# Three up-weight loads on ScalarE's queue and a summed mean in an S5 scan with a GeGLU block

## The chip, the cores and the metric

One core of one Trainium2 chip. The metric is the device time of one execution in microseconds; the time before is the median of three runs.

The engines of the core work through queues of their own, each in order: TensorE (PE, matmuls and transposes into PSUM), VectorE (DVE), ScalarE (ACT), GpSimd (POOL) and SyncE (SP, which here only issues DMA transfers). They wait for each other by semaphores. A DMA transfer is issued by an instruction in some engine's queue and then runs on DMA engines beside it. ScalarE can issue transfers too: such an instruction stands in the same order as its arithmetic.

## What is computed

The input x has 2048 tokens of 512 features. Each token is layer-normalized; the result feeds a diagonal complex state-space scan (S5) and a GeGLU feed-forward block, whose SiLU gates the scan's output:

```
xn = _layernorm(x, axis=-1)
# S5: 512 complex states
Lam_bar = exp(dt * Lam);  dt = exp(log_dt)
Bu = einsum("bld,pd->blp", xn, ((Lam_bar - 1) / Lam)[:, None] * Bmat)
h  = Lam_bar * h + Bu[:, t, :]          # for t in 0..2047
s  = 2 * einsum("blp,dp->bld", h, Cmat).real + xn * Dskip
# GeGLU: 512 -> 1376 -> 512
g  = silu((gelu(xn @ w_gate) * (xn @ w_up)) @ w_down)
return x + s * g
```

All tensors are bfloat16.

## The kernel before

The tokens are cut into four slabs of 512, each slab into four tiles of 128 tokens. For a slab TensorE computes the up and gate products (`gate_tile`, L536), the down product (`down_pair`, L564), the input product of the scan (`half`, L615) and its output product (`y_part`, L579). The scan runs on VectorE, turned by a table of angles before and after (`half`, L627 to L659). ScalarE moves most products from PSUM to SBUF. The weights have four row tiles of 128 features (k = 0 to 3) and three column pieces of 512, 512 and 352 (c = 0 to 2).

The first slab is handled apart, since everything is still on its way. `center` takes the mean off each of its tiles: for tile 0 VectorE sums 320 of the 512 columns (L414, into `ma`) and ScalarE the other 192 (L411, into `mb`), and VectorE subtracts both in two pieces of 256 columns (L418). For tiles 1 to 3 ScalarE sums all columns (L423) and VectorE subtracts (L424). `head_t` transposes the centered tile on TensorE (L387 for tile 0 in two halves, L400 for the others) and copies it back into `xcT` (L391, L393, L402). `up_rows` then multiplies one tile, one row tile and one column piece at a time (L462), so that TensorE can start with the row tiles that have landed; the 352-column piece is done with all four row tiles at once (`first_w`, L499), and so are the gate products. The products are scaled with 1/sqrt(var) when they leave PSUM (L471, L505).

The weights come in pieces over SyncE's queue: three token tiles, then up row tile 0 (two halves of 512), the 352-column piece of all row tiles, row tile 1 and so on, the gate weights and the second slab (`load_x`, `load_w`, `load_slab`: L296, L287, L291). The three rows of parameters (log_dt, the imaginary and the real part of Lambda) are loaded over ScalarE's queue (L333), transposed (L672, L673), and make the angles (`angles`, L683 to L689) and the table (`tables`, L708).

No order is left to a compiler. Each call of `dve`, `acts`, `pe`, `pool` or `dma` adds a step with what it reads and writes to `Plan` (the costs given there have no effect on the program). `ORDER` is the order in which the steps are written out, and so each engine's own order; `SLOTS` says which buffer or PSUM bank each step's tile takes (six banks for whole products in `ps`, two in `pp`). The framework adds the semaphores. Each transfer signals its end on one of eight of them.

TensorE begins with seven products of constants (`dummies`, L375). The output of slab s is made tile by tile: `y_part` puts the skip term into the bank (L575), adds eight products (L579), multiplies by the gate (L585), adds x (L586) and stores (L589). The last tile of the last slab is done in two halves of 256 columns.

Of the kernel before, what the change touches and what calls it, by code (L numbers as in the profile page):

```python
# [45 lines left out]
)  # L46
SLOTS = {
# [4 lines left out]
    ),  # L52
    "pp": (
# [95 lines left out]
def kernel(  # L149
# [18 lines left out]
    P = 128  # L168
# [27 lines left out]
    def sb(name, shape, dt=BF16):  # L196
        return consts.tile(shape, dt, name=name)
# [722 lines left out]
```

## Time and profile before

| | |
|---|---|
| runs | 179.06, 178.76, 178.73 us |
| median | 178.76 us |
| span of the profiled execution | 176.9 us |
| median less span | 1.86 us |
| TensorE busy | 172.1 us (97%) |
| VectorE busy | 154.6 us (87%) |
| ScalarE busy | 132.6 us (75%) |
| moved by DMA | 18.66 MB |

The span runs from the first to the last instruction of one execution under the profiler; its own time outside the span isn't recorded, so the runs' median less the span stands for it. In the lines that follow, a timeline row gives start, duration in us, engine, source line, operation, tile written and read, shape and count; the bracket says how long the engine had been idle and what ended that. "SPq" and "ACTq" are issues of transfers. "PE" rows overlap: a matmul's duration is longer than the time until the next one starts. A row by stretches gives the stretch, its length, busy us and count of each engine (PE, PE's weight loads, DVE, ACT, POOL), TensorE's clock, the DMA engines' busy share and GB/s. The chain of waits follows the work that ended last back to the start: start, duration, who.

### The profile page before, as it was taken

What the parts mean: (1) busy time and instruction counts of PE and PEld (TensorE: products, weight loads), DVE (VectorE), ACT (ScalarE), POOL (GpSimd) and SP (SyncE); (2) the same over time, 40 slices, a digit from 0 to 9 for tenths busy, and PEclk for the clock granted to TensorE, in tenths of its full rate; (3) what the DMA queues carried; (4) which work ended last, traced back from release to release, by engine and by line L of the source; (5) the groups of instructions that cost most, each with busy time, mean ns of one, the idle gap of its engine ahead of it and who ended that gap; (6) DMA issues with size and microseconds to landing.
All of it is one profiled execution on the core that took longest, in us unless ns stands there. A gap on an engine that the chain in (4) does not pass through costs nothing.

```text
span 176.9 us, 2418 instructions
## 1 busy us (share of the span) xinstructions
PE 172.1 (97%) x834; PEld 82.3 (47%) x849; DVE 154.6 (87%) x253; ACT 132.6 (75%) x246; POOL 10.9 (6%) x25
## 2 busy tenths in 40 slices
PE   8999999999999999999999999999999999999992
PEld 2554544454454444444444444444444444444451
DVE  3743799999999988999999699999999999999343
ACT  6679999989999999956697665735898860793310
POOL 2640500000200000011000000000000000000000
PEclk9999999999999999999999999999999999999999
DMA  5999999997092730040057050063007300550531
GB/s 150 285 347 247 160 288 189 305 217 158 8 193 43 138 62 4 0 82 0 0 115 150 2 111 0 0 126 70 0 11 154 87 0 4 129 123 0 113 119 30
DMA packets 48467, 18.66 MB, mean 105 GB/s; under 512 B 40296, under 2 KB 48328, under 8 KB 48456
## 3 DMA queue, kind: packets, MB, share of 16 engines
q1 hardware_dynamic: 48432, 18.52, 46.7%
q8 instruction: 6, 0.10, 0.2%
q14 instruction: 5, 0.04, 0.1%
q10 hardware_dynamic: 24, 0.00, 0.0%
HBM read 6.46 MB, written 2.10 MB: 48 GB/s over the span
## 4 chain that ended last, share of the span: by engine, by line
PE 94%; DMA 2%; SPq 1%; issue 1%; DVE 0%
PE bank L536 31%; PE bank L564 21%; PE bank L615 16%; PE bank L579 16%; PE bank L499 7%; PE bank L462 3%; DMA wu<-in_B_w_up_dram 2%; SPq L296 1%; SPq L287 0%; DVE yg L585 0%; DVE ot L586 0%; PE bank L400 0%
## 5 line engine op out<-in xcount | busy, mean ns | idle before, releaser
L536 PEld LDWEIGHTS <-xnT 128*128 128x128 bf16 x288 | 28.1, 98 | 29.4
L564 PE MATMUL bank<-wd,atT 128*128 128x512 bf16 (+1 forms) x174 | 40.2, 379 | 0.1
L536 PE MATMUL bank<-wu,xnT 128*128 128x512 bf16 (+1 forms) x140 | 31.9, 356 | 0.1
L536 PE MATMUL bank<-wg,xnT 128*128 128x512 bf16 (+1 forms) x139 | 31.7, 356 | 0.3
L615 PE MATMUL bank<-xnT,BT 128*128 128x512 bf16 x128 | 30.9, 379 | 0.1
L646 DVE TENSOR_TENSOR_SCAN Fs<-rho,ini,W 128x512 bf16<-128x512 f32 x24 | 29.8, 1272 | 0.1
L579 PE MATMUL bank<-C,hst 128*128 128x512 bf16 (+1 forms) x134 | 29.7, 366 | 0.1
L564 PEld LDWEIGHTS <-atT 128*128 128x128 bf16 (+1 forms) x176 | 17.2, 98 | 20.3
L539 ACT ACTIVATE ubA<-bank 128x512 bf16<-128x512 f32 x24 | 14.6, 614 | 8.8 <-PE bank L536 8.3
L617 ACT ACTIVATE U<-bank 128x512 bf16<-128x512 f32 x32 | 19.1, 622 | 1.7 <-PE bank L615 1.7
L579 PEld LDWEIGHTS <-hst 128*128 128x128 bf16 x136 | 13.3, 98 | 14.0
L615 PEld LDWEIGHTS <-BT 128*128 128x128 bf16 x128 | 12.5, 98 | 14.3
L627 DVE TENSOR_TENSOR Q<-U,tab 128x4096 bf16<-128x4096 bf16 x8 | 18.3, 2287 | 0.7 <-ACT tab L715 0.6
L539 ACT ACTIVATE gtA<-bank 128x512 bf16<-128x512 f32 x24 | 14.8, 616 | 5.3 <-PE bank L536 4.6
L627 DVE TENSOR_TENSOR Q<-Fs,tab 128x4096 bf16<-128x4096 bf16 x8 | 18.3, 2285 | 0.1
L567 ACT ACTIVATE g<-bank 128x512 f32<-128x512 f32 x16 | 9.2, 594 | 12.1 <-PE bank L564 12.1
L585 DVE TENSOR_TENSOR yg<-bank,g 128x512 bf16<-128x512 f32 (+1 forms) x17 | 11.1, 655 | 5.0 <-PE bank L579 4.6
L539 ACT ACTIVATE ubB<-bank 128x352 bf16<-128x352 f32 x12 | 5.7, 475 | 6.6 <-PE bank L536 5.5
L838 ACT ACTIVATE junk<-x_tok 128x512 bf16<-128x512 bf16 x16 | 10.2, 649 | 0.0
L499 PE MATMUL bank<-wg,W 128*128 128x512 bf16 (+1 forms) x47 | 9.7, 356 | 0.1
L843 ACT ACTIVATE xna<-x_tok,nb,rs 128x512 bf16<-128x512 bf16 x12 | 9.6, 876 | 0.0
L575 ACT ACTIVATE bank<-sk 128x512 f32<-128x512 bf16 (+1 forms) x17 | 9.5, 577 | 0.1
(121 smaller groups left out, 190.0 us busy)
## 6 DMA issues: line engine op xcount, KB each, us to landing
out_dram<-ot SPq DMA_DIRECT2D x15, 128.0 KB, 1.8
x_tok<-in_A_x_dram SPq DMA_DIRECT2D x3, 512.0 KB, 5.6
wd<-in_B_w_down_dram SPq DMA_DIRECT2D x1, 1280.0 KB, 7.1
wg<-in_B_w_gate_dram SPq DMA_DIRECT2D x1, 864.0 KB
wu<-in_B_w_up_dram SPq DMA_DIRECT2D x6, 128.0 KB, 3.3
x_tok<-in_A_x_dram SPq DMA_DIRECT2D x4, 128.0 KB, 2.2
wg<-in_B_w_gate_dram SPq DMA_DIRECT2D x1, 512.0 KB, 7.8
wu<-in_B_w_up_dram SPq DMA_DIRECT2D x1, 352.0 KB, 3.9
```

The lines of the kernel that those rows point to most:

```text
L499: T.matmul(ps[:, 0 : b - a], lhsT=xcT[:, k, m * P : (m + 1) * P], rhs=wt[:, k, a:b], start=(k == 0), stop=(k == KT - 1))
L536: T.matmul(ps[:, 0 : b - a], lhsT=xnT[:, s % 2, m, k, :], rhs=wt[:, k, a:b], start=(k == 0), stop=(k == KT - 1))
L539: acts(b - a, lambda: act(out=dst, in_=ps[:, 0 : b - a], func=AF.Copy if up else AF.Gelu_apprx_tanh), [key], [ok], table=None if up else " ...
L564: T.matmul(ps[:], lhsT=atT[:fs, k, iT * P : (iT + 1) * P], rhs=wd[:fs, k, :], start=(k == 0), stop=(k == NFT - 1))
L579: T.matmul(ps, lhsT=hst[s % 2][:, j // NPT, j % NPT, m * P : (m + 1) * P], rhs=C2[:, j // NPT, j % NPT, c0:c1], start=False, stop=(j == 2 ...
L585: dve(w, lambda: V.tensor_tensor(out=yg[iy][:, 0:w], in0=ps, in1=g2[ig][:, c0:c1], op=ALU.mult), [key, ("g2", gg)], [("yg", gy)])
L615: T.matmul(ps[:], lhsT=BT[:, ri, k, pt * P : (pt + 1) * P], rhs=xnT[:, s % 2, :, k, :], start=(k == 0), stop=(k == KT - 1))
L617: acts(512, lambda q=q, ri=ri, ps=ps: act(out=U[ui][:, ri, q, :], in_=ps[:], func=AF.Copy), [key], [("U", ug, q, ri)])
L627: dve(4096, lambda: V.tensor_tensor(out=Qf, in0=src.unsqueeze(1).to_broadcast(WQ), in1=table, op=ALU.mult), reads, ["Q"], rate=2.0)
L646: pl.add(DVE, 1.12 if s == 0 else 1.185, lambda ri=ri, q=q, pt=pt, first=first: V.tensor_tensor_scan(out=Fs[:, ri, q, :], data0=rho[:, pt ...
L838: acts(512, lambda i=i, fn=fn, sc=sc, m=m: act(out=junk()[:], in_=x_tok[:, s * M + m, :], func=fn, scale=sc, accum_out=sx[:, s, i, m : m + ...
L843: acts(512, lambda m=m: act(out=xn[m], in_=x_tok[:, s * M + m, :], func=AF.Identity, scale=rs[:, s, m : m + 1], bias=nb[:, s, m : m + 1]), ...
```

## The change

Four things are changed:

- Up row tile 0 (both halves) and the second half of row tile 1 are loaded by ScalarE's queue instead of SyncE's.
- Of the parameter rows only log_dt stays on ScalarE's queue, ahead of these loads; the other two go to SyncE's.
- For tile 0, VectorE first adds the two partial means into a new `mc` (128x1), and then subtracts one scalar instead of two.
- `ORDER` and `SLOTS` are replaced as wholes: every engine's order and the choice of buffers differ over the whole kernel. There is one step more (693 for 692).

```
-    def load_w(nm, k0, k1, c0, c1, end, landed):
+    def load_w(nm, k0, k1, c0, c1, end, landed, act_queue=False):
         w, r = w_of[nm]
-        dma_sp(end, landed, lambda: nc.sync.dma_start(out=w[:, k0:k1, c0:c1], in_=r[:, k0:k1, c0:c1]),
-               [(nm, k, c) for k in range(k0, k1) for c in range(3) if c0 <= CH[c][0] < c1])
+        keys = [(nm, k, c) for k in range(k0, k1) for c in range(3) if c0 <= CH[c][0] < c1]
+        if act_queue:
+            dma(ACT, 0.43, landed - end, lambda: A.dma_start(out=w[:, k0:k1, c0:c1], in_=r[:, k0:k1, c0:c1]), writes=keys)
+            return
+        dma_sp(end, landed, lambda: nc.sync.dma_start(out=w[:, k0:k1, c0:c1], in_=r[:, k0:k1, c0:c1]), keys)
...
-    load_w("wu", 0, 1, 0, W1, 2.53, 4.4)
-    load_w("wu", 0, 1, W1, W2, 3.0, 4.95)
+    load_w("wu", 0, 1, 0, W1, 2.53, 4.4, act_queue=True)
+    load_w("wu", 0, 1, W1, W2, 3.0, 4.95, act_queue=True)
     load_w("wu", 1, 2, 0, W1, 3.47, 5.5)
-    load_w("wu", 1, 2, W1, W2, 3.94, 6.05)
+    load_w("wu", 1, 2, W1, W2, 3.94, 6.05, act_queue=True)
...
-        first = [dma(ACT, 0.48, 1.7, lambda t=t, v=v: A.dma_start(out=t, in_=v.rearrange("(k p) -> k p", p=P)),
-                     writes=[("pv", i)], rank=900.0, not_before=0.8, after=first)]
+        qe, qn = (A, ACT) if i == 0 else (nc.sync, SP)
+        dma(qn, 0.3, 2.4, lambda t=t, v=v, qe=qe: qe.dma_start(out=t, in_=v.rearrange("(k p) -> k p", p=P)), writes=[("pv", i)])
...
+    mc = sb("mc", [P, 1], FP32)
...
+            dve(1, lambda: V.tensor_tensor(out=mc[:, 0:1], in0=ma[:, 0:1], in1=mb[:, 0:1], op=ALU.add), [("ma", 0), "mb"], ["mc"])
             for i in range(2):
                 c0, c1 = i * HD, (i + 1) * HD
-                dve(HD, lambda c0=c0, c1=c1: V.tensor_scalar(out=xn[0][:, c0:c1], in0=x[:, c0:c1], scalar1=ma[:, 0:1], scalar2=mb[:, 0:1],
-                                                             op0=ALU.subtract, op1=ALU.subtract),
-                    [("x", 0, 0), ("ma", 0), "mb"], [("xc", 0, i)], rate=2.3)
+                dve(HD, lambda c0=c0, c1=c1: V.tensor_scalar(out=xn[0][:, c0:c1], in0=x[:, c0:c1], scalar1=mc[:, 0:1], scalar2=None, op0=ALU.subtract),
+                    [("x", 0, 0), "mc"], [("xc", 0, i)], rate=2.3)
```

The new heads of the queues that load, in order:

```
ACT: log_dt row; up k0 c0, up k0 c1; up k1 c1; partial mean of tile 0 (now L415)
SP:  x tiles 0, 1, 2; up k1 c0; up 352 columns, all k; x tile 3; up k2 c0; up k2 c1; Lambda rows;
     up k3 (1024 columns); gate 864 columns; gate 512 columns; second slab; Dskip;
     first xnT, then both transposed B; third and fourth slab; second xnT
```

In the new order TensorE has ten up products of row tiles 0 and 1 ahead of the 352-column products (six before), and the parameters' transposes come after those. VectorE's end of the order is: slab 2 tile 0 (multiply, add), then the last half tile of the last tile (multiply, add). The changed kernel's lines lie three or four further down: L415 is the partial mean on ScalarE, L420 the new sum, L423 the subtraction, L391 the transposes of tile 0, L503 the 352-column and first gate products, L583 the output products.

More of the change, by code (lines that the diff above doesn't have):

```diff
@@ L48 @@
     "ps": (
[3 rows of a table removed]
[3 rows of a table added]
     ),
     "pp": (
-        0, 1, 0, 1, 0, 1, 0, 1, 0, 0, 0, 1, 0, 1, 0, 1, 0, 1, 0, 1, 1, 0, 1, 0, 1, 1, 1, 0, 0, 0, 0, 1, 1, 0, 1, 0, 1, 0, 1,
+        0, 0, 1, 0, 0, 1, 1, 0, 1, 0, 0, 0, 1, 1, 0, 1, 0, 0, 1, 0, 0, 1, 1, 0, 1, 0, 1, 0, 0, 0, 1, 1, 0, 1, 0, 0, 0, 0, 0,
     ),
     "U": (
-        0, 1, 0, 2, 0, 1, 0, 2,
+        0, 1, 0, 2, 0, 1, 2, 0,
     ),
     "g2": (
-        5, 0, 1, 4, 3, 0, 4, 2, 2, 0, 1, 5, 3, 1, 4, 5,
+        4, 1, 0, 3, 0, 5, 3, 2, 5, 4, 5, 1, 2, 3, 1, 0,
     ),
     "at": (
-        2, 0, 1, 3, 2, 1, 0, 0, 0, 1, 2, 3, 2, 3, 0, 1,
+        0, 1, 3, 2, 0, 3, 2, 1, 3, 1, 1, 0, 2, 1, 2, 0,
     ),
     "gtA": (
-        0, 0, 1, 1, 0, 1, 0, 1, 1, 0, 0, 0, 1, 1, 0, 0,
+        1, 0, 0, 1, 0, 0, 0, 1, 0, 1, 1, 0, 0, 1, 1, 1,
     ),
     "gtB": (
-        1, 1, 0, 0, 0, 0, 1, 1, 1, 0, 0, 0, 0, 1, 0, 1,
+        0, 1, 0, 0, 1, 1, 1, 0, 1, 0, 0, 1, 0, 1, 0, 1,
     ),
     "ubA": (
-        0, 1, 0, 0, 1, 1, 1, 0, 0, 0, 1, 1,
+        0, 0, 1, 1, 0, 1, 1, 0, 1, 1, 0, 0,
     ),
     "ubB": (
-        0, 0, 1, 1, 1, 0, 0, 1, 0, 0, 1, 0,
+        0, 1, 0, 1, 1, 1, 0, 1, 0, 1, 0, 1,
     ),
     "yg": (
-        0, 0, 1, 1, 0, 1, 0, 1, 0, 1, 1, 0, 0, 0, 1, 0, 1, 0,
+        0, 1, 0, 1, 0, 0, 1, 1, 1, 0, 1, 0, 0, 1, 1, 0, 1, 0,
     ),
     "ot": (
-        1, 1, 1, 0, 1, 0, 0, 0, 0, 0, 0, 1, 1, 0, 1, 0, 1,
+        0, 1, 1, 0, 0, 0, 0, 1, 1, 0, 1, 0, 0, 0, 1, 0, 1,
     ),
     "sk": (
-        2, 3, 0, 1, 5, 7, 4, 6, 0, 1, 3, 2, 5, 4, 6, 7,
+        1, 2, 0, 3, 4, 7, 5, 6, 1, 2, 3, 0, 4, 6, 5, 7,
     ),
     "atT": (
-        0, 1, 3, 0, 1, 1, 3, 2, 0, 3, 2, 1, 1, 2, 3, 0,
+        0, 1, 3, 2, 3, 2, 2, 1, 3, 3, 1, 0, 2, 0, 2, 1,
     ),
```

54 rows, old and new, of tables (ORDER, SLOTS) are left out of this document.

## The prediction

> **What bounds the kernel now.** I read the page first (busy time, chain by engine), then the chain of waits in order of time, then the timeline by engine at both ends, then busy time by stretches.
>
> ```profile
> span 176.9 us, 2418 instructions
> ...
> PE 94%; DMA 2%; SPq 1%; issue 1%; DVE 0%
> ```
>
> TensorE carries 94% of the chain. The chain in order of time says from where:
>
> ```profile
> 3.06 3.89 DMA wu<-in_B_w_up_dram
> ...
> 6.99 1.35 PE bank L499 x8
> 8.35 0.43 PE bank L462 x2
> ...
> 172.01 1.76 PE bank L579 x16
> ```
>
> From 6.99 to 173.77 (172.01 + 1.76) no piece belongs to another engine. So three terms make the time: how much TensorE work is left at 6.99 (head), whether TensorE is starved later (body), and what follows its last matmul (tail). The span is 176.9, the median of the runs 178.76 us; the 1.86 us around the span stay as they are, and differences are added to 178.76.
>
> The head before, first the loads, then ScalarE, then VectorE, then TensorE's groups up to 7 us (count, busy us, mean ns):
>
> ```profile
> 0.79 0.55 ACTq L333 DMA_DIRECT2D pv<-in_A_log_dt_dram  x1
> ...
> 2.11 1.93 SPq L287 DMA_DIRECT2D wu<-in_B_w_up_dram  x4
> ...
> 3.90 0.66 PE L387 MATMUL bank<-ident,xna 128*128 128x128 bf16 x4
> ```
>
> ```profile
> 2.88 0.36 ACT L411 ACTIVATE junk<-x_tok 128x192 bf16<-128x192 bf16 x1 [0.67 <-DMA x_tok<-in_A_x_dram]
> 3.15 0.19 ACT L411 ACTIVATION_READ_ACCUMULATOR junk<-x_tok 128x1 f32 x1
> 3.44 0.63 ACT L423 ACTIVATE junk<-x_tok 128x512 bf16<-128x512 bf16 x1
> 3.97 0.19 ACT L423 ACTIVATION_READ_ACCUMULATOR junk<-x_tok 128x1 f32 x1
> 4.06 0.61 ACT L423 ACTIVATE junk<-x_tok 128x512 bf16<-128x512 bf16 x1
> ```
>
> ```profile
> 3.49 0.60 DVE L418 TENSOR_SCALAR xna<-x_tok,ma,mb 128x256 bf16<-128x256 bf16 x2
> 4.19 0.35 DVE L424 TENSOR_SCALAR xna<-x_tok,ma 128x512 bf16<-128x512 bf16 x1
> 4.46 0.28 DVE L391 COPY W<-bank 128x256 bf16<-128x256 bf16 x1
> ```
>
> ```profile
> L462 PE MATMUL bank<-wu,W 128*128 128x512 bf16 x6 | 1.6, 381 | 0.0
> L400 PE MATMUL bank<-ident,xna 128*128 128x128 bf16 x8 | 0.8, 222 | 0.1
> L387 PE MATMUL bank<-ident,xna 128*128 128x128 bf16 x4 | 0.7, 302 | 0.0
> ```
>
> ScalarE's part of the first mean starts when tile 0 arrives (2.88), the transposes at 3.90. By 6.99 TensorE has done twelve transposes and only six up products: it was short of tiles and weights.
>
> **The change part by part.** The listing of the changed program, with the semaphore that each instruction waits for, shows two waits that the diff doesn't:
>
> ```
> ACT 4 DMACopy wu_66<-in_B_w_up_dram 128x512 x2
> ACT 5 DMACopy wu_66<-in_B_w_up_dram 128x512 [waits DMAHW0_49]
> ACT 6 Activation junk1_116,mb_138<-x_tok_63 128x192
> DVE 2 TensorScalarPtr yg0_110,ma_137<-x_tok_63 128x320 [waits DMAHW0_49]
> PE 60 Matmult bank7_124<-wu_66,W_92 128x352 [waits DMAHW6_49]
> SP 9 DMACopy wu_66<-in_B_w_up_dram 128x1024 [waits DMAHW6_49]
> ```
>
> Loads share eight completion semaphores, and a load that reuses one waits for its last user. ScalarE's third load reuses that of token tile 0, so it goes out only when tile 0 has landed, and the partial mean stands behind it in ScalarE's order.
>
> *Head, ScalarE.* Such an issue on ScalarE isn't shown. Bounds: 0.43 (SyncE's four take 1.93, 0.04 between them) and 0.55 (ScalarE's first parameter row). I take 0.43 + 0.04, the same form of load. The parameter row and two loads end near 2.3; the third goes out from 2.88, the mean starts at 3.35 instead of 2.88, its accumulator is read by 3.81 (before 3.34), and VectorE follows 0.15 later, as it did at 3.49: 3.96.
>
> *Head, VectorE.* The new 128x1 sum isn't shown; the nearest row has 4 columns:
>
> ```profile
> 9.41 0.15 DVE L679 TENSOR_TENSOR a<-pf,dt__149 128x4 f32<-128x4 f32 x1
> ```
>
> With 0.04 to the next, dependent instruction: 4.15. The subtraction of one scalar from 256 columns lies between half of L424 (0.18: one scalar, 512 columns, 0.35) and L418 (0.34: two scalars, 256 columns, the second half entering 0.26 after the first); I take 0.21, near L424, which has the same form. First half 4.36, transposes 4.42 (they came 0.07 after L418's first half): 0.52 later than 3.90.
>
> *Head, TensorE.* The new order puts the copy of the first half ahead of tile 1's subtraction. Two transposes need 0.29 (0.22 and the next behind it), the copy 0.28: 4.75 to 5.03, first up product 5.13. Tile 1's mean is read at 4.63 (0.47 after the 4.16 of before), its subtraction runs 4.96 to 5.31, its transposes start at 5.37; tile 2's, 0.62 behind, at 6.02 once two products are through. Their copies (at most twice 0.28) end by 6.4 and 7.0, in time for products at 6.46 and 7.10. A product issues every 0.216 (8.35: two in 0.43), and so do four transposes (as many columns). So 5.13 one product, 5.37 transposes, two products, 6.02 transposes, seven products: the 352-column product begins at **7.75** with ten up products done. Before, it began at 6.99 with six and the parameters' two small transposes (0.1): 6.99 + 4 x 0.216 - 0.1 = 7.75. Head: **0.0**, from -0.47 (the mean isn't held) to +0.25 (issue 0.55, subtraction 0.34).
>
> So TensorE's early want of weights goes, and the wait takes the same amount back. The memory side has little to give (the last two columns are the DMA engines' busy share and GB/s):
>
> ```profile
> 3.00:4.00 1.00, 1.00 (x5) 0.11 (x2) 0.89 (x4) 0.91 (x4) 0.00 (x0) 1.00 0.90 264
> 4.00:5.00 1.00, 0.95 (x9) 0.45 (x8) 0.85 (x4) 1.00 (x5) 0.00 (x0) 1.00 0.78 194
> ```
>
> Only a fifth of one microsecond stands idle. The Trainium skill, DMA: Bandwidth & Descriptors, section "Issuing engines are not separate DMA queues", says that a second issuing engine saves issue time alone, since all transfers run on the same 16 engines. The shares agree, and by that rule alone the head would come out near 0 too.
>
> *Body.* TensorE's total is unchanged; after 7.75 it ends at 173.75 if it is fed. The times at which TensorE wants something, below, are sums of its rows along the new order from 7.75 on. I followed the hand-offs with these rows (ScalarE, then SyncE):
>
> ```profile
> 13.74 1.83 ACT L471 ACTIVATE at<-bank,rs 128x512 bf16<-128x512 f32 x3
> 15.59 1.28 ACT L505 ACT_TABLE_LOAD   x1
> ```
>
> ```profile
> 16.30 3.03 SPq L436 DMA_TRANSPOSE xnT<-xna  x1
> 19.38 2.42 SPq L314 DMA_TRANSPOSE BT<-in_A_B_im_dram  x1
> ...
> 25.91 2.98 SPq L436 DMA_TRANSPOSE xnT<-xna  x1
> ```
>
> ```profile
> DMA to landing us min/median/max: 4.9/5.3/5.8
> ```
>
> Tightest is ScalarE behind its table load. Its last piece of work before it ends near 16.1, the table is there at 17.4, eight evictions at most 0.57 apart (L471: three in 1.83) bring it to 21.97, and the one that frees the next bank ends at 22.4 to 22.5, where TensorE wants it (22.47). The second slab's transposed tokens leave at 25.9 as before and land 4.9 to 5.8 later (30.8 to 31.7); both orders want them at 31.45. The B transposes now follow the first xnT: the first takes xnT's place (16.30) and is wanted at 23.07, the second leaves as before (19.38) and is wanted at 25.66; by 5.8 both have room. Body: **+0.1**, from 0 to +0.4, since several margins are zero.
>
> *Tail.* In the new order VectorE has a whole other tile (slab 2, tile 0) right ahead of the last half tile:
>
> ```profile
> 169.74 0.69 DVE L585 TENSOR_TENSOR yg<-bank,g 128x512 bf16<-128x512 f32 x1
> 170.47 0.43 DVE L586 TENSOR_TENSOR ot<-yg,x_tok 128x512 bf16<-128x512 bf16 x1
> ...
> 173.79 0.42 DVE L585 TENSOR_TENSOR yg<-bank,g 128x256 bf16<-128x256 f32 x1
> ```
>
> TensorE ends that tile eight half products (0.88) before its last, at 172.9; yg starts at 172.97, ot 0.73 later at 173.70, and the last yg can enter 0.33 behind it (0.43 less the overlap): 174.03 instead of 173.79, and all behind it 0.24 later. Tail: **+0.24**, from 0 (the store hides it) to 0.4.
>
> The parameters' way over SyncE and the later memsets cost nothing, because VectorE waits for the second slab's tokens until 16.14 in any case; without that cover the chain of angles would cost some 0.3:
>
> ```profile
> 16.14 0.69 DVE L356 BATCH_NORM_STATS2 st<-x_tok 128x6 f32<-128x512 bf16 x1 [4.09 <-DMA x_tok<-in_A_x_dram]
> ```
>
> Sum: 178.76 + 0.0 + 0.1 + 0.24 = 179.10; with 0.05 for the loads behind the second wait (a tenth of rival 3's price), **179.15** (own range 178.85 to 179.45).
>
> **The rivals.**
> 1. *The mean isn't held.* ScalarE issues its third load without delaying the mean. For it: at 0.79 it issued while its table was still loading. Against: it would have to run past a semaphore. Head -0.47: 179.10 - 0.47 = 178.63.
> 2. *That, and a tail that hides.* The store of the other tile overlaps the last: 178.63 - 0.24 - 0.1 = 178.3.
> 3. *The last up rows come late: slower.* SyncE issues row tile 3 (SP 9) only once the 352-column load has landed, and the gate weights behind it. Such waits held nobody before; that load took 3.89 (3.06 to 6.95). Issued at 2.58 it lands at 6.5 to 7.0, and row tile 3 needs as long as any up load:
>
> ```profile
> DMA to landing us min/median/max: 2.2/3.5/3.9
> ```
>
> It lands between 8.7 and 10.9 and is wanted at 10.35; it decides from there on. Price up to 0.55: 179.7. Against: 3.5 is the time in a full queue, and at 7 us the queue has just run empty.
> 4. *TensorE's fast rate comes later: slower.*
>
> ```profile
> 0.76 3.15 PE L375 MATMUL bank<-const-bfloat16-1.0 128*128 128x512 bf16 x7 [0.76 <-PEq L904]
> ```
>
> Seven warm-up products take 3.15 (0.45 each, twice 0.216), the first transposes 0.30 and later ones 0.22: the fast rate comes after about 4.2. With TensorE idle from 3.91 to 4.42 it may come one such stretch (3.4) later, near 7.9; ten products at half rate until then cost 1.4: 180.5. The Trainium skill, TensorE: Matmul & The Clock Gate, Part 1, speaks of a free-running window of 3.4 us that has to be busy. The trace agrees with the length; whether the gap spoils the window no run shows.
>
> **How the numbers follow.** Forecast 0.45, rival 1 0.22, rival 2 0.10, rival 3 0.17, rival 4 0.06. About 0.2% (0.36 us) is what a measurement here can tell from no change. Faster (below 178.40): rival 2 and a third of rival 1, 0.17. Slower (above 179.12): 0.25 of the forecast, rivals 3 and 4, 0.48. The same: 0.35. The range 178.4 to 180.0 leaves out rival 4 and most of rival 2.
>
> **What would show it.** Right: the partial mean (now L415) starts near 3.35, the first transposes (L391) at 4.4, the first 352-column product (L503) at 7.7, TensorE's last matmul ends at 173.8 to 174.0, the last ot starts near 174.5. Wrong: the mean still starts at 2.9 (rival 1); TensorE idles ahead of the row tile 3 products near 10 us (rival 3); products after 5 us are 0.43 apart (rival 4); or TensorE has an idle stretch of over 0.3 us after 23 us.

## The result and the profile after

The changed kernel is slower: 181.09 us (median of 11 runs, 180.61 to 182.30) against 178.93 for the kernel before in the same runs, a ratio of 1.0112 (95%: 1.0079 to 1.0145). Two of the ten runs of one kernel below, parts_old_order (181.77 and 183.21 us), count as slow, being more than 1.5% over its fastest: its median of 180.42 holds them, and without them it is 180.15. The profiled execution of the changed kernel has a span of 179.1 us, 2.2 more than before. The page shows that TensorE no longer carries the chain alone:

```profile
span 179.1 us, 2413 instructions
...
PE 67%; ACT 14%; DVE 11%; DMA 4%; issue 3%; DVEq 0%; ACTq 0%
```

The chain of waits in order of time (start, duration, who) says where the others come in:

```profile
2.88 4.21 DMA wu<-in_B_w_up_dram
7.13 1.67 PE bank L466 x7
...
14.97 0.69 ACT at L475
...
38.69 0.50 ACT U L621
...
140.95 0.58 DVE yg L589
...
174.89 0.70 DVE yg L589
```

Three stretches of the new chain ahead of TensorE's last product are not TensorE's: a load at the start, ScalarE from 14.97 to 39.2, and VectorE ahead of 144.5. TensorE's timeline shows what each costs:

```profile
4.29 0.48 PE L391 MATMUL bank<-ident,xna 128*128 128x128 bf16 x4 [0.38 <-DVE xna L423]
4.96 0.39 PE L466 MATMUL bank<-wu,W 128*128 128x512 bf16 x1 [0.19 <-DVE W L395]
...
5.89 0.39 PE L404 MATMUL bank<-ident,xna 128*128 128x128 bf16 x4
7.13 1.67 PE L466 MATMUL bank<-wu,W 128*128 128x512 bf16 x7 [0.86 <-DMA wu<-in_B_w_up_dram]
8.64 1.36 PE L503 MATMUL bank<-wu,W 128*128 128x352 bf16 x8
9.83 0.59 PE L466 MATMUL bank<-wu,W 128*128 128x512 bf16 x2
10.36 0.17 PE L676 MATMUL bank<-ident,pv 4*128 4x4 bf16 x1
...
10.49 0.82 PE L466 MATMUL bank<-wu,W 128*128 128x512 bf16 x3
...
39.23 1.02 PE L540 MATMUL bank<-wu,xnT 128*128 128x512 bf16 x4 [0.20 <-ACT U L621]
...
144.49 1.02 PE L540 MATMUL bank<-wg,xnT 128*128 128x512 bf16 x4 [0.31 <-ACT gtA L543]
...
172.91 2.76 PE L583 MATMUL bank<-C,hst 128*128 128x512 bf16 x16
```

A row lasts until its last product has drained (0.38 for one of 512 columns), while the next could have been issued after 0.216. So an idle time in the brackets understates the loss by some 0.16. The three waits cost 0.86 + 0.16 = 1.02, 0.20 + 0.16 = 0.36 and 0.31 + 0.16 = 0.47 us. The first can be read from the starts too: four transposes from 5.89 take 0.22 and end at 6.11, and the next product starts at 7.13.

| term | predicted | measured | how |
|---|---|---|---|
| head | 0.0 | 1.02 | 352-column products at 8.64; before, with the same work done, 6.99 + 4 x 0.216 - 0.23 = 7.62 (the parameters' transposes, 10.26 to 10.49 here) |
| body | 0.1 | 0.88 | TensorE's last matmul ends at 175.67 (172.91 + 2.76), before at 173.77: 1.90, less 1.02 |
| tail | 0.24 | 0.27 | last yg at 175.96, before at 173.79: 2.17, less 1.90 |

Of the body's 0.88, the waits at 39.2 and 144.5 make 0.36 + 0.47 = 0.83. The head is that of one execution: of four further kernels below whose head is the same but for one product of constants more in one of them, three reach the 352-column products at 8.36 to 8.69, so it costs 0.7 to 1.1 in them too; the fourth, gate_sooner, is told below.

The tail's rows on VectorE, which is still busy with the other tile when TensorE is done at 175.67:

```profile
174.89 0.69 DVE L589 TENSOR_TENSOR yg<-bank,g 128x512 bf16<-128x512 f32 x1 [2.08 <-PE bank L583]
175.62 0.43 DVE L590 TENSOR_TENSOR ot<-yg,x_tok 128x512 bf16<-128x512 bf16 x1
175.96 0.42 DVE L589 TENSOR_TENSOR yg<-bank,g 128x256 bf16<-128x256 f32 x1
```

The wait at 39.2 comes from ScalarE's queue:

```profile
37.82 0.78 ACT L842 ACTIVATE junk<-x_tok 128x512 bf16<-128x512 bf16 x1
38.34 0.35 ACT L842 ACTIVATION_READ_ACCUMULATOR junk<-x_tok 128x1 f32 x1
38.43 0.75 ACT L621 ACTIVATE U<-bank 128x512 bf16<-128x512 f32 x1
```

Such a sum over 512 columns of the third slab takes 0.61 with its read-out (37.82 to 38.43). The new order has eight of them ahead of this eviction, the old one four in the same stretch, and the eviction frees the bank that TensorE wants next.

The wait at 144.5 is a loop over three engines, first VectorE's row, then ScalarE's:

```profile
141.78 0.68 DVE L522 TENSOR_TENSOR at<-gtA,ubA 128x1024 bf16<-128x1024 bf16 x1
```

```profile
142.54 1.28 ACT L543 ACT_TABLE_LOAD   x1 [3.16 <-DVE at L522]
143.84 1.08 ACT L543 ACTIVATE gtA<-bank 128x512 bf16<-128x512 f32 x2
```

VectorE's gate product reads a gate buffer (`gtA`) that ScalarE's next gate eviction overwrites. ScalarE has been idle for 3.16 us, yet it loads its table only after that wait, so the 1.28 us come on top.

### The profile page after: what moved, and what is told of

The parts are those of the page before. It is cut to its first block, busy times and chain, and to the rows that moved or that the text cites. A ratio compares the mean times of both kernels' runs of the same rounds, so it can differ in the third digit from the quotient of the medians.

```text
span 179.1 us, 2413 instructions
## 1 busy us (share of the span) xinstructions
PE 172.1 (96%) x833; PEld 82.3 (46%) x849; DVE 154.8 (86%) x254; ACT 130.2 (73%) x244; POOL 13.7 (8%) x25
## 4 chain that ended last, share of the span: by engine, by line
PE 67%; ACT 14%; DVE 11%; DMA 4%; issue 3%; DVEq 0%; ACTq 0%
PE bank L540 21%; PE bank L568 18%; PE bank L583 14%; PE bank L619 10%; DVE Fs L650 4%; PE bank L466 3%; ACT junk L842 3%; ACT gtA L509 3%; DVE Q L631 3%; DMA wu<-in_B_w_up_dram 2%; ACT U L621 2%; ACT at L475 2%; ACT xna L847 2%; DMA x_tok<-in_A_x_dram 1%; DVE yg L589 1%
## 5 line engine op out<-in xcount | busy, mean ns | idle before, releaser
L540 PE MATMUL bank<-wu,xnT 128*128 128x512 bf16 (+1 forms) x144 | 32.8, 357 | 0.3 <-ACT U L621 0.2
L619 PE MATMUL bank<-xnT,BT 128*128 128x512 bf16 x128 | 31.5, 379 | 0.0
L583 PE MATMUL bank<-C,hst 128*128 128x512 bf16 (+1 forms) x131 | 29.0, 366 | 0.3
L621 ACT ACTIVATE U<-bank 128x512 bf16<-128x512 f32 x32 | 19.6, 633 | 7.9 <-PE bank L619 7.9
L583 PEld LDWEIGHTS <-hst 128*128 128x128 bf16 x136 | 13.3, 98 | 14.0
L842 ACT ACTIVATE junk<-x_tok 128x512 bf16<-128x512 bf16 x16 | 11.1, 720 | 0.0
L503 PE MATMUL bank<-wg,W 128*128 128x512 bf16 (+1 forms) x47 | 10.1, 356 | 0.1
L466 PE MATMUL bank<-wu,W 128*128 128x512 bf16 x31 | 8.3, 379 | 1.1 <-DMA wu<-in_B_w_up_dram 0.9
```

What stands on the lines that cost most here:

```text
L466: T.matmul(ps[:], lhsT=xcT[:, k, m * P : (m + 1) * P], rhs=wu[:, k, a:b], start=(k == 0), stop=(k == KT - 1))
L540: T.matmul(ps[:, 0 : b - a], lhsT=xnT[:, s % 2, m, k, :], rhs=wt[:, k, a:b], start=(k == 0), stop=(k == KT - 1))
L583: T.matmul(ps, lhsT=hst[s % 2][:, j // NPT, j % NPT, m * P : (m + 1) * P], rhs=C2[:, j // NPT, j % NPT, c0:c1], start=False, stop=(j == 2 ...
L619: T.matmul(ps[:], lhsT=BT[:, ri, k, pt * P : (pt + 1) * P], rhs=xnT[:, s % 2, :, k, :], start=(k == 0), stop=(k == KT - 1))
L621: acts(512, lambda q=q, ri=ri, ps=ps: act(out=U[ui][:, ri, q, :], in_=ps[:], func=AF.Copy), [key], [("U", ug, q, ri)])
L842: acts(512, lambda i=i, fn=fn, sc=sc, m=m: act(out=junk()[:], in_=x_tok[:, s * M + m, :], func=fn, scale=sc, accum_out=sx[:, s, i, m : m + ...
```

## The experiments

My theory (T) after reading the trace was that the head waits for weights that land late, that the new order makes the two later waits by itself, and that the tail is as predicted. The rivals are named in the expectations, which were written before the runs. An edit of the order is shown by step numbers: in ORDER, steps 0 to 2 and 7 are the loads of the token tiles, 3 and 4 those of up row tile 0, 5 and 6 of row tile 1 (6 is ScalarE's third load), 8 and 9 of row tile 2, 10 of row tile 3, 11 the 352-column load, 25 to 27 the parameter rows, 30 the partial mean. Unless said otherwise the base is the changed kernel. "Ratio" is against the kernel before in the same runs; the changed kernel's is 1.0112.

| kernel | median us | ratio (95%) | span |
|---|---|---|---|
| load_after_mean | 182.35 | 1.0180 (1.0135 to 1.0225) | 180.1 |
| up11_on_sync | 180.42 | 1.0074 (1.0053 to 1.0095) | 178.6 |
| order_alone | 180.59 | 1.0084 (1.0063 to 1.0105) | 178.5 |
| parts_old_order | 180.42 | 1.0078 (1.0044 to 1.0112) | 177.2 |
| sum_later | 181.24 | 1.0132 (1.0096 to 1.0168) | 178.9 |
| gate_sooner | 181.33 | 1.0126 (1.0094 to 1.0157) | 179.4 |
| tail_halves | 182.02 | 1.0170 (1.0142 to 1.0198) | 179.2 |
| eight_warmups | 180.89 | 1.0106 (1.0085 to 1.0127) | 178.8 |
| parts_old_order_warm | 179.49 | 1.0028 (1.0015 to 1.0041) | 177.7 |
| mc_alone | 179.11 | 0.9999 (0.9984 to 1.0014) | 177.4 |
| old_order_two | 179.67 | 1.0047 (1.0021 to 1.0073) | 177.4 |
| three_mended | 179.45 | 1.0033 (1.0016 to 1.0050) | 177.4 |
| wide_load_later | 181.57 | 1.0110 (0.9915 to 1.0305) | 180.7 |

### Is it the held mean or the late load?

**load_after_mean**

```
-    ... 3, 2, 4, 5, 6, 30, 45, 11, 7 ...
+    ... 3, 2, 4, 5, 30, 6, 45, 11, 7 ...
```

> Kernel: the changed one, with ScalarE's third load (up row tile 1, second half) put behind the partial mean in ScalarE's order; nothing else. Theory T (late weights): of the changed kernel's 2.16 us, 1.03 are TensorE's wait for this load, which lands at 7.09 because the 352-column load (360 KB) was issued ahead of it; 0.36 (at 39.2) and 0.47 (at 144.5) are waits that the new order makes by itself; 0.26 is the tail. By T the mean starts at 2.9 and the first transposes at 3.9, but the load still lands at 7.1 or later (it now waits for token tile 1), TensorE still waits for it, and the time stays within 0.2 us of the changed kernel's 181.09 (up to 0.4 slower). Rival H (the hold): the 0.39 by which the mean is late is what costs; then this kernel is 0.4 us faster, 180.7.

The mean now starts at 2.92 and the transposes at 4.07, but the load (chain of waits) lands later still, and TensorE (timeline) waits for it:

```profile
3.48 4.60 DMA wu<-in_B_w_up_dram
```

```profile
5.67 1.16 PE L466 MATMUL bank<-wu,W 128*128 128x512 bf16 x2
...
8.11 1.67 PE L466 MATMUL bank<-wu,W 128*128 128x512 bf16 x7 [1.05 <-DMA wu<-in_B_w_up_dram]
```

Issued 0.60 later, it lands at 8.08 instead of 7.09. Undoing the hold gained nothing, and rival H is out; in the changed kernel, too, TensorE still waits 0.86 for the load after the held mean. The loss is larger than T allowed (span +1.0, up to 0.4 expected), and all of it is the load's: the row at 8.11 stands 0.98 later than that at 7.13.

**up11_on_sync**

```
-    load_w("wu", 1, 2, W1, W2, 3.94, 6.05, act_queue=True)
+    load_w("wu", 1, 2, W1, W2, 3.94, 6.05)
```

> Kernel: the changed one, with up row tile 1's second half issued by SyncE, behind its first half and ahead of the 352-column load. By T the load lands near 5.5 to 5.9 instead of 7.09, TensorE has no wait for it (its 352-column products begin at 7.2 to 7.7 instead of 8.64), and the time falls by 0.9 to 1.3 us to 179.8 to 180.2; the waits at 39 and 144 us stay, a us earlier. Rival H: only the hold goes, -0.4, 180.7. Rival O (the loss lies in the new order alone, and the head only moves waits about): less than 0.3 us comes off, since the later waits grow by what the head gains.

TensorE doesn't wait for this load any more; its 352-column products start at 7.94, 0.70 sooner. They were expected from 7.2 on, and what now sets the time is token tile 2, for whose sum ScalarE waits; before the change that sum started at 4.06 without a wait:

```profile
5.03 0.63 ACT L427 ACTIVATE junk<-x_tok 128x512 bf16<-128x512 bf16 x1 [0.78 <-DMA x_tok<-in_A_x_dram]
```

```profile
7.94 1.36 PE L503 MATMUL bank<-wu,W 128*128 128x352 bf16 x8
```

The later waits are there as T has them, at 38.70 and 143.95, 0.53 and 0.54 sooner than in the changed kernel. The other 0.16 goes between 10.45 and 12.12, where four transposes and six products take 1.67, in the changed kernel 1.52 (11.15 to 12.67). With 0.5 of the span T's size was missed by about half; its mechanism is what the rows show.

**wide_load_later**

```
-    ... 45, 11, 7, 8, 9 ...
+    ... 45, 7, 8, 11, 9 ...
```

> Kernel: the changed one, with the 352-column load (360 KB) put behind token tile 3 and the first half of row tile 2 in SyncE's order. ScalarE's third load now shares its semaphore with token tile 1, so it goes out, and the mean starts, some 0.5 later than in the changed kernel (near 3.4 and 3.8). Theory T (order on the 16 DMA engines): with 128 to 256 KB instead of 360 ahead of it the third load lands 2.8 to 3.4 us after its issue instead of 4.21. Rival Q (a load that ScalarE issues in the middle of the stream is slow in itself, whatever is ahead): 4.0 to 4.6 again. The time is no test here: the mean comes later and so do the 352 columns; 180.5 to 181.8.

The profile's summary of ScalarE's three loads (the changed kernel, then this one):

```profile
DMA to landing us min/median/max: 3.0/3.6/4.2
```

```profile
DMA to landing us min/median/max: 3.1/3.1/3.1
```

The summary holds the landings that the profile ties to an issue, two of the three in each kernel. Here both come 3.1 us after the issue, that of the third load, issued at 3.58, too; in the changed kernel the 4.2 is the third load's. So a load of ScalarE's isn't slow in itself, and rival Q is out.

What counts is all that is ahead of it, not the 352-column load alone (352 KB; 360 in the expectations, in thousands of bytes). Added up from the issues and landings, 768 KB of token tiles and weights issued earlier have not landed here when the third load goes out, 864 KB in parts_old_order and parts_old_order_warm (below), where the 352-column load is among them too, and 992 KB in the changed kernel and in load_after_mean. The load takes 3.1 us here, 3.4 and 3.7 with 864 KB, 4.2 and 4.6 with 992 KB, and 3.9 to 4.3 in four further kernels with 992 KB. Nor does it wait until the 352 columns are there: in the changed kernel it lands at 7.09, and they, issued at 2.58, took 5.0.

### Parts and order apart

**order_alone**

```
-    load_w("wu", 0, 1, 0, W1, 2.53, 4.4, act_queue=True)
+    load_w("wu", 0, 1, 0, W1, 2.53, 4.4)
 the other two loads likewise
...
-        qe, qn = (A, ACT) if i == 0 else (nc.sync, SP)
+        qe, qn = A, ACT
...
-    ... 25, 1, 3 ... 9, 26, 27, 10 ...
+    ... 25, 26, 27, 1, 3 ... 9, 10 ...
```

> Kernel: the changed kernel's order, buffers and summed mean, but all loads of weights issued by SyncE and all three parameter rows by ScalarE, as before the change. By T the mean isn't held and row tile 1 comes ahead of the 352 columns, so TensorE waits less in the head: only for the 352-column load, which now goes out behind everything at 4.4 and lands near 8; 180.1 to 180.8, with the two later waits in place. Rival H: 180.7. Rival I (issuing from ScalarE saves SyncE's time and is worth that much; without it the head gets worse): 181.4 or more. Rival O: 181.0 within 0.2.

180.59, within T's range; in the profile TensorE's last row stands 0.54 earlier than in the changed kernel. SyncE alone serves the new order no worse than both queues. TensorE's wait for weights is still there, smaller, and its 352-column products begin at 8.09. T named the wrong load for it: it isn't the 352-column load, for which TensorE doesn't wait here, but one of the 128 KB loads ahead of it:

```profile
6.14 0.38 PE L466 MATMUL bank<-wu,W 128*128 128x512 bf16 x1 [0.59 <-DMA wu<-in_B_w_up_dram]
```

Both later waits stand at 38.70 and 143.95, so they belong to the order. Rival I is out. H forecast the same time; it falls by load_after_mean.

**parts_old_order**

```
 ORDER, SLOTS: those of before, with the new sum (step 32, later steps one number up) and,
 with the parameters' transposes (38, now 39) moved too,
-    ... 25, 1, 26, 2, 27, 3, 4, 30, 31, 11, 44, 32, 6 ... 62, 38, 71, 70, 10, 39 ...
+    ... 25, 1, 2, 3, 4, 6, 30, 31, 11, 26, 27, 45, 32 ... 63, 72, 71, 10, 39, 40 ...
```

> Kernel: everything of the change but its order and buffers: the order of before, with the three loads on ScalarE's queue in the place that they have in the changed kernel, two parameter rows on SyncE's behind the 352-column load, the parameters' transposes put just ahead of their copy, and the summed mean. By T the old order needs six products ahead of the 352 columns, which are loaded early here, and row tile 1 only later, so nothing waits for the third load: 178.6 to 179.2, with no wait of TensorE near 39 or 144 us. Rival H: 179.3 (the mean is held all the same). Rival I' (loads from ScalarE's queue are slow in themselves): 179.9 or more.

The profiled execution agrees with T: 177.2, no wait of TensorE behind the head, 352-column products at 7.29 (before: 6.99, with the same work ahead). The median doesn't, and by the time alone this would be rival I'; but in the profile ScalarE's loads take 2.6 to 3.4 us, no longer than SyncE's before (2.2 to 3.9), so they are not slow in themselves. The ten runs lie between 179.02 (the profiled one) and 183.21. That is the widest spread so far, and two further kernels were made for it (below); what the later runs lost no profile shows.

**mc_alone**

```
 on the kernel before:
+            dve(1, lambda: V.tensor_tensor(out=mc[:, 0:1], in0=ma[:, 0:1], in1=mb[:, 0:1], op=ALU.add), [("ma", 0), "mb"], ["mc"])
-  ... scalar1=ma[:, 0:1], scalar2=mb[:, 0:1], op0=ALU.subtract, op1=ALU.subtract) ...
+  ... scalar1=mc[:, 0:1], scalar2=None, op0=ALU.subtract) ...
```

> Kernel: the one before with the summed mean alone. By the measured rows the new sum (0.16) costs more than the two-scalar subtraction saves (0.06): the transposes of tile 0 come 0.10 to 0.15 later than 3.90; behind them TensorE waited 0.24 for the 352-column load at 6.99 in any case, so the time stays within 0.15 us of before. Theory W adds that the idle stretch of 0.1 may delay the fast rate in some runs. Rival M (the sum costs its full 0.19 all the way, since the two-scalar subtraction isn't dearer): +0.2.

No change (0.9984 to 1.0014). The transposes start at 4.01, 0.11 later, and TensorE waits for the 352 columns behind them in any case:

```profile
7.50 1.35 PE L500 MATMUL bank<-wu,W 128*128 128x352 bf16 x8 [0.26 <-DMA wu<-in_B_w_up_dram]
```

```profile
4.36 0.63 ACT L424 ACTIVATE junk<-x_tok 128x512 bf16<-128x512 bf16 x1 [0.32 <-DMA x_tok<-in_A_x_dram]
```

These rows also show how far the same loads in the same queues move between executions: the 352 columns come 0.5 later than in the kernel before (6.99), and the sum of token tile 2, for which ScalarE now waits, 0.3 later (4.06).

### The two later waits and the tail

These edits are worth less than the runs' spread, so TensorE's positions in the profile decide, not the medians. By the medians all three kernels are slower than the changed one (181.24, 181.33 and 182.02 for 181.09), so none of the gains that T forecast came out in time.

**sum_later**

```
-    ... 441, 298, 141, 313, 303, 201, 314 ... 318, 364, 304 ...
+    ... 441, 298, 141, 313, 201, 314 ... 318, 364, 303, 304 ...
```

> Kernel: the changed one, with the last of ScalarE's eight sums over the third slab's tokens that stand ahead of the scan's eviction at 38.4 us moved some five us later in ScalarE's order. Theory T: TensorE's wait at 39.2 comes from ScalarE's queue, which is full from 15 us on and holds these sums (0.61 each) ahead of an eviction whose bank TensorE wants; without one of them the eviction comes 0.61 sooner and the 0.36 go: span 178.7 to 178.8 (179.1), time 0.3 to 0.4 lower, and TensorE's wait near 144 us stays. Rival O (a wait taken away here comes back at the next tight place): the wait at 144 grows by what goes here, time within 0.15 of 181.09. Rival D (ScalarE is late because of transfers): the wait at 39 stays.

TensorE's wait at 39 is gone, so ScalarE's queue was its cause. But only part of the 0.36 is kept. The row that stands at 144.49 in the changed kernel starts at 144.29, and 0.10 of these 0.20 come from the head (352-column products at 8.54 for 8.64). In between a hand-off takes over in which ScalarE waits for VectorE:

```profile
44.16 0.60 ACT L543 ACTIVATE gtA<-bank 128x512 bf16<-128x512 f32 x1 [0.26 <-DVE at L522]
```

It comes at 44.24 in the changed kernel, 0.08 later, so it hardly moves with what ScalarE gains. That is rival O, though at 44, not at 144.

**gate_sooner**

```
-    ... 553, 539, 550, 551, 536, 533, 607, 623, 552 ...
+    ... 553, 550, 551, 536, 607, 623, 539, 533, 552 ...
```

> Kernel: the changed one, with two skip terms on VectorE (slab 3, tiles 2 and 3; 0.33 each, at 138.3 and 141.5 us) put behind the two gate products at 141.9 and 142.5. Theory T: VectorE is full from 122 to 142 us; its gate product frees the buffer that ScalarE's next gate eviction writes, and ScalarE's table load of 1.28 stands behind that wait, then comes the eviction that frees TensorE's bank. With 0.66 less ahead of it the table load starts near 141.9 and TensorE's wait of 0.47 at 144.5 goes; span 178.6 to 178.7, time 0.4 to 0.5 lower. Rival P (the table load doesn't depend on the wait, something else holds it): the wait at 144.5 stays and the time with it.

The wait at 144.5 is gone; down products and gate products follow each other (11 x 0.216 = 2.38 from 142.45):

```profile
142.45 2.54 PE L568 MATMUL bank<-wd,atT 128*128 128x512 bf16 x11
144.82 1.03 PE L540 MATMUL bank<-wg,xnT 128*128 128x512 bf16 x4
```

The execution is longer all the same, for a reason in its head:

```profile
7.31 2.29 PE L466 MATMUL bank<-wu,W 128*128 128x512 bf16 x7
9.43 0.31 PE L503 MATMUL bank<-wu,W 128*128 128x352 bf16 x1
```

The seven products that took 1.67 at 7.13 take 2.29 here, and the 352 columns begin 0.79 later. TensorE's last row starts at 173.25, 0.34 after that of the changed kernel: 0.81 more at 40.04, 0.47 less at 144. That the wait isn't gone merely because TensorE comes late is shown by three_mended (below), which has the same edit and an early head; there the gate products follow without a wait too:

```profile
142.85 1.03 PE L540 MATMUL bank<-wg,xnT 128*128 128x512 bf16 x4
```

**tail_halves**

```
-    ... 679, 669, 689, 661 ... 670, 690, 671, 691, 675, 680, 692, 672 ... 641, 683, 573, 642, 643, 644, 684 ...
+    ... 679, 669, 661 ... 670, 671, 675, 680, 672 ... 641, 689, 683, 573, 642, 643, 644, 690, 691, 692, 684 ...
-    ot = [sb(f"ot{i}", [P, D]) for i in range(2)]
+    ot = [sb(f"ot{i}", [P, D]) for i in range(2)] + [at[0][:, 0:D]]
```

> Kernel: the changed one, with both halves of the last tile at the very end of TensorE's and VectorE's order, so that no whole tile stands right ahead of the last half; the store that this half would have waited for gets an output buffer of its own. Theory T: the last multiply enters as soon as TensorE is done instead of 0.23 to 0.26 later: span 178.8 to 178.9, time 0.2 to 0.3 lower. Rival S: the extra half on VectorE and its store take the same room: no change within 0.1.

No gain: by the profile, rival S. Its "no change" doesn't fit the time, though: four of the five runs lie at 181.93 to 182.10, only the profiled one (180.93) near the changed kernel's 181.09, and what the four lost stays open. Two halves after a whole tile leave the last one behind just as much:

```profile
175.34 0.42 DVE L589 TENSOR_TENSOR yg<-bank,g 128x256 bf16<-128x256 f32 x1
175.80 0.29 DVE L590 TENSOR_TENSOR at<-yg,x_tok 128x256 bf16<-128x256 bf16 x1
176.01 0.42 DVE L589 TENSOR_TENSOR yg<-bank,g 128x256 bf16<-128x256 f32 x1
```

TensorE ends at 172.10 + 3.64 = 175.74, the last yg enters at 176.01, 0.27 later, as in the changed kernel. In the old order a down product (2.38) stands between the last whole tile and the halves, and gives VectorE its time.

### When TensorE gets fast

**eight_warmups**

```
-    dummies(7)
+    dummies(8)
```

> Kernel: the changed one, with eight products of constants at the start instead of seven. The changed kernel's runs lie 1.7 us apart (180.61 to 182.30), those of before 0.47 but for one; in the profile of the kernel with the load behind the mean TensorE's up products took 0.63 instead of 0.38 up to 6.6 us. Theory W: TensorE's idle stretch from 3.9 to 4.3, which the kernel before doesn't have, sometimes delays its fast rate by a stretch. With an eighth product it is busy to 4.2 or 4.3: the runs close to within 0.6 of each other and the median falls by 0.2 to 0.4, the lowest time stays. Rival N: the spread has other causes and stays; the median within 0.15 of 181.09.

Six runs between 180.65 and 181.30 (0.65 apart, 1.7 in the changed kernel), median 0.2 lower: near W, but with half the runs no proof. Nor did the eighth product bridge the stretch: in the profile TensorE is still idle for 0.18 ahead of its transposes at 4.29.

**parts_old_order_warm**

```
-    dummies(7)
+    dummies(9)
```

> Kernel: the one with everything of the change but its order (parts_old_order), with nine products of constants at the start instead of seven. That kernel's ten runs lay between 179.02 and 183.21 us, its profile (the fastest) 177.2. Theory W: TensorE's idle stretch from 3.9 to 4.3, which the held mean makes, delays its fast rate in some executions (in the profile of the kernel with gates sooner, which has the same stretch, up products took 0.6 until 7 us and the 352-column products began 0.8 later). Nine products bridge it (to 4.3 to 4.4): all runs within 0.8 of each other, median 179.0 to 179.5. Rival N: the spread has other causes: the runs stay over 2 us apart and the median above 180.

Twelve runs between 179.27 and 180.24, median 179.49 for 180.42 without the two products. Rival N is out. The profile shows that bridging doesn't make the rate come early: though TensorE is busy without a gap from 0.76 on, the rate came after 6.3 us here, with single products 0.63 and 0.56 long, and four of them 1.04 behind that:

```profile
5.41 0.63 PE L466 MATMUL bank<-wu,W 128*128 128x512 bf16 x1
...
6.26 0.56 PE L466 MATMUL bank<-wu,W 128*128 128x512 bf16 x1
...
6.88 1.04 PE L466 MATMUL bank<-wu,W 128*128 128x512 bf16 x4
```

What the two products take away, to judge by the runs, is the later cases; that the long runs without them were executions with a late rate is argued, since none of those has a profile. Where there is one, without the bridge, the fast rate was there at 4.29 in the changed kernel (four transposes in 0.48; 0.61 where it is slow; 0.38 idle ahead of them), near 6.6 in load_after_mean (0.17 idle), near 8.6 in gate_sooner (0.43 idle) and latest, near 9.6, in wide_load_later (1.08 idle). The last two are estimates: seven products at the fast rate take 1.67, gate_sooner's 2.29 and these 2.52, so that three and four of them came 0.43 apart instead of 0.216:

```profile
7.87 2.52 PE L466 MATMUL bank<-wu,W 128*128 128x512 bf16 x7
```

The Trainium skill, TensorE: Matmul & The Clock Gate, Part 1, says that the activity window is free-running, so that the moment of the change differs from run to run. It puts that at 500 ns to either side of some 4 us; the profiles agree that the moment moves, but by far more: from before 4.3 to 9.6 us for nearly the same start. How much of a gap spoils a window they don't show: sum_later, with 0.47 idle, has the fast rate at 4.37, and the kernel with the bridge gets it later than that.

### Towards a faster kernel

**old_order_two**

```
 on the kernel before:
+    load_w("wu", 0, 1, 0, W1, 2.53, 4.4, act_queue=True)
+    load_w("wu", 0, 1, W1, W2, 3.0, 4.95, act_queue=True)
 and the last two parameter rows on SyncE, the parameters' transposes (38) later:
-    ... 25, 1, 26, 2, 27, 3, 4, 30, 31, 11, 44 ... 62, 38, 71, 70, 10, 39 ...
+    ... 25, 3, 1, 4, 2, 30, 31, 11, 26, 27, 44 ... 62, 71, 70, 10, 38, 39 ...
```

> Kernel: the one before, with only up row tile 0 loaded from ScalarE's queue behind the log_dt row, the other two parameter rows on SyncE's queue behind the 352-column load, and the parameters' transposes just ahead of their copy; the old order, the old subtraction, the second half of row tile 1 on SyncE's queue. Nothing holds the mean (2.9), the 352-column load goes out at 2.1 instead of 3.06 and lands near 6 instead of 6.95. Theory T: TensorE's wait of 0.24 ahead of its first 352-column product goes: 0.1 to 0.3 us faster than before. Rival O: the old order is tuned to that wait, no change within 0.1. Rival I' (loads from ScalarE's queue delay the tokens behind them): 0.2 or more slower.

Slower (1.0021 to 1.0073), as rival I' has it. In the profile, no product waits for weights, but tile 2's transposes wait for its subtraction; before, they ran at 5.21:

```profile
5.78 0.40 PE L404 MATMUL bank<-ident,xna 128*128 128x128 bf16 x4 [0.59 <-DVE xna L428]
```

ScalarE's sum of token tile 2 starts at 4.61 instead of 4.06, and the 352-column products at 7.44 instead of 6.99. That the tile shares the DMA engines with weights that ScalarE issued at 1.37, ahead of it, fits: it takes 2.2 us from issue to landing before, 2.6 in mc_alone, and 2.6 to 3.8 in the twelve kernels here with such weights ahead. But this execution (179.18) doesn't explain the slower median: mc_alone's profiled one is as long (179.20, 352 columns at 7.50), and its median is that of before. The loss lies in runs of up to 181.15 without a profile, and its cause stays open. Their spread, 2.2 us, came without a gap between the products of constants and the transposes (3.83) in the profiled execution.

**three_mended**

```
-    load_w("wu", 1, 2, W1, W2, 3.94, 6.05, act_queue=True)
+    load_w("wu", 1, 2, W1, W2, 3.94, 6.05)
-    dummies(7)
+    dummies(8)
 and the order of sum_later and gate_sooner
```

> Kernel: the changed one with four of the edits tried alone: the second half of row tile 1 on SyncE's queue, one sum later on ScalarE, two skip terms later on VectorE, eight products of constants. If the pieces add (-0.54 for the load, -0.47 at 144 us, -0.10 to -0.35 for the sum), the span is 177.8 to 178.1 and the time 1.1 to 1.4 us below the changed kernel's: 179.7 to 180.0. What stays of the 2.2 over the kernel before is then 0.27 of tail and 0.5 to 0.8 in the head and at VectorE's hand-off near 44.8 us. Rival O: they don't add, 180.3 or more.

179.45, span 177.4: 1.7 us of the span's 2.2 are gone, somewhat more than the pieces add up to, because the head is whole in this execution (352-column products at 7.59, by the count above 7.62). It is among the fastest of ten: six runs lie at 179.22 to 179.48, four at 180.00 to 180.06. By the ratios (1.0033 for 1.0112) 1.4 us are gone, the upper end of what the pieces add up to. It doesn't beat the kernel before (1.0016 to 1.0050). No kernel here does.

## Why the prediction was wrong

The side that it held likelier (slower, 0.48) came true; the size, 179.15 with 178.4 to 180.0, did not. The side was partly luck: only the tail's 0.27 of the 2.2 us came the way the forecast has it. By its own steps:

- *Head, ScalarE*: right. The third load goes out at 2.88 for 0.34 and the mean starts at 3.26 (3.35 forecast):

```profile
2.88 0.34 ACTq L289 DMA_DIRECT2D wu<-in_B_w_up_dram  x1
3.26 0.36 ACT L415 ACTIVATE junk<-x_tok 128x192 bf16<-128x192 bf16 x1 [1.05 <-DMA x_tok<-in_A_x_dram]
```

- *Head, VectorE*: right. The sum takes 0.16 (0.15 + 0.04 with the gap), both subtractions together 0.48; the transposes start at 4.29 (4.42).
- *Head, TensorE*: **the step that failed.** First up product at 4.96 (5.13), tile 1's transposes at 5.22 (5.37), tile 2's at 5.89 (6.02): all a little sooner than forecast. Then the prediction let seven products follow without asking when the weights of row tile 1 are there. It priced the third load by its issue alone and not by its landing. From 2.88, its own landing row (median 3.5, longest 3.9) gives 6.4 to 6.8, later than the 6.24 at which its count wanted them; in the run it was 7.09. An estimate by bytes comes nearer: with the 992 KB ahead of it and its own 128 it ends 1.15 MB of transfers, which at the rate of the kernel before from 3 to 7 us (264, 194, 323 and 357 GB/s, 285 on average) take 4.0 us, until 6.9. Issued ahead of the 352 columns (up11_on_sync, order_alone), the load keeps TensorE waiting no more. Head 0.0 became 1.02 (0.89 against its own 7.75, which had the parameters' transposes at 0.1 instead of 0.23).
- *Body*: **the second step, a term of the sum mis-sized.** The prediction saw hand-offs without margin and gave them 0.1, at most 0.4; they cost 0.88. The place that it named, ScalarE behind its table load at 22.4, cost nothing. The two places that did were those at 39.2 and 144.5; sum_later and gate_sooner removed each. The second needs a table load that waits behind a semaphore, which the prediction's durations had left out.
- *Tail*: right in mechanism and size (0.24; measured 0.27 and unmoved by tail_halves).
- *Parameters over SyncE, the later memsets, the new sum*: nothing, as forecast; mc_alone shows it for the sum.
- *Rivals 1 and 2* (the mean isn't held): it was held, and where it wasn't (load_after_mean) nothing was gained.
- *Rival 3* (row tile 3 late): half right. SyncE did wait for the 352-column load and issued row tile 3 only at 7.56, later than forecast, since that load took 5.0 where the prediction took over the 3.89 of before (6.5 to 7.0). The DMA engines' busy share in that stretch (the last two columns are share and GB/s) fell to a third of what it was; before the change, then after:

```profile
7.00:8.00 1.00, 1.00 (x7) 0.67 (x7) 0.56 (x3) 0.16 (x1) 0.83 (x3) 1.00 1.01 262
```

```profile
7.00:8.00 1.00, 0.87 (x5) 0.39 (x5) 0.78 (x3) 0.15 (x3) 0.43 (x2) 1.00 0.35 118
```

  TensorE, itself a us late, didn't wait for it.
- *Rival 4* (fast rate later): not in the profiled execution, but in those of other kernels with this head: 0.79 in gate_sooner, where 1.4 was forecast. Given 0.06, it deserved more.
- The rule of the Trainium skill (DMA: Bandwidth & Descriptors, "Issuing engines are not separate DMA queues") was read as "no gain". The runs show a loss as well: with more KB ahead of it the third load took longer (3.1 to 4.6 us), and the sum of token tile 2, which has weights of ScalarE's ahead of it, went from 4.06 to 4.71 here and 5.03 in up11_on_sync (mc_alone, without them, has 4.36, so a part of that is spread).

## What to carry to other kernels

Where a load moves to another queue, write down for every piece when it is issued, what is queued ahead of it on the DMA engines, and when it is wanted; a second queue changed the order of arrival here, and found the DMA engines busy already (shares of 0.78 to 1.05 from 3 to 7 us before, 0.91 to 1.09 after). Price hand-offs with no margin as costs and not as risks: two of them made 0.8 of 2.2 us here, and taking one away handed most of its gain to the next. The moment at which TensorE gets fast moved by over 5 us between executions with nearly the same start, so look at several executions before a difference below 1% is believed.

## What was not expected of the hardware

- TensorE's fast rate came between 4.3 and some 9.6 us after the start in profiles of nearly the same kernel. The clock that the profile records (the third column from the end) reads 1.00 also where a product takes 0.63, as here in load_after_mean; only the rows' durations show it:

```profile
5.00:6.00 1.00, 1.00 (x6) 0.68 (x6) 0.41 (x3) 1.00 (x4) 0.00 (x0) 1.00 1.05 332
```

- A table load (1.28) is held by the semaphore that the activation behind it waits for: at 142.54 it started after ScalarE had been idle for 3.16. The activation followed at 143.84, 1.30 after the load's start.
- The same 128 KB load from ScalarE's queue landed after 3.1, 4.21 or 4.60 us, with 768 KB, 992 KB and 992 KB issued ahead of it and not yet landed.
